# A sliding-window attention and channel-mix kernel: first loads in 512-byte runs, and a searched order of GpSimd's loads

## The chip, the cores and the metric

One core of a Trainium2 chip runs the whole program. The metric is device time in microseconds (us) of one execution; three runs of the kernel before gave a median of 232.38 us (231.59 to 232.47).

## The reference

```python
def _attn_ref(q, k, v):                     # q, k, v: (8, 8, 576, 64), float32
    scores = scale * np.matmul(q, k.transpose(0, 1, 3, 2))
    rel = pos[:, None] - pos[None, :]
    bias = slopes[:, None, None] * (-np.abs(rel))[None, :, :]
    mask = (rel >= 0) & (rel < 128)
    scores = np.where(mask, scores + bias[None], -1000000000.0)
    ...
    return np.matmul(attn, v)               # attn: softmax of scores

def _moe_ref(x, mu_k, mu_r, w_k, w_v, w_r): # x: (8, 576, 512), heads side by side
    x_prev = np.concatenate([zeros, x[:, :-1, :]], axis=1)
    xk = mu_k * x + (1.0 - mu_k) * x_prev
    xr = mu_r * x + (1.0 - mu_r) * x_prev
    k = np.maximum(xk @ w_k, 0.0)           # w_k: (512, 1024)
    v = k * k @ w_v                         # w_v: (1024, 512)
    return (1.0 / (1.0 + np.exp(-(xr @ w_r)))) * v
```

Causal attention over a window of 128 positions with a bias that falls with distance, and then a channel mix of its output.

## The kernel before

**The work.** Eight batches of 576 positions are four tiles of 128 and a tail of 64; the eight heads are four pairs. For a pair, q and k are brought to "head dimension on partitions" by transposes on TensorE (quarter-array ones at L1053, half-array ones at L804, or, for batches 6 and 7, by DMA transposes on SP's queue). Then come the scores (L693, 12 matmuls of 64 rows, the two heads side by side), their Exp on ScalarE (L707), a multiplication by a mask on VectorE (L720), and attend (L749, 18 matmuls against v with a column of ones, which gives the sums). VectorE divides (L755, L760), TensorE transposes back (L787, L804), a copy (L663) brings the result to `xt`, and VectorE makes the shifted mixes xk and xr (L847, L854). The channel mix runs in chunks of 256 to 512 positions: L958 (w_k), Relu on ScalarE (L965), the square (L929, L931), L976 (w_r), Tanh (L983), L992 (w_v), the product on VectorE (L997) and the store (L1022, the last piece L1016).

**The first batch** is done in two parts. Part 0 is its first 256 rows. `first_load` (L511) fetches q and k in float32 by SP's and ScalarE's hardware queues (L517) into `stage`. For pairs 0 and 1 a partition takes two neighbouring rows, which is a run of 512 bytes; VectorE casts them (L663 `qx<-qx`), and TensorE transposes them in bf16 (L1100). Pairs 2 and 3 (`FT`) come together, row by row, in runs of 256 bytes, and TensorE transposes them in float32 (L1097) with no cast. Part 1, the rest of the rows, is loaded by GpSimd. In this batch the bias goes in by matmuls (L680, `dist` and `sid`), whose operands GpSimd and VectorE make first: iota (L404), `ident` (L408), the cuts of `dist` (L412, L415), `sid` (L635), copies of `dist` (L633). All transposes need `ident`. Ninety matmuls on zeros (L654) fill TensorE while it waits.

**The order of work** is planned: each piece of work is a node with a duration, predecessors, buffers that it takes and gives back (`Hold`), and a priority for each engine. `Plan.run` (L106) places them one after the other, and each engine runs its list in that order. The priorities come from `rank` (L355), with fitted numbers in `LEAD` and `SHIFT`. `pe_key` (L98) lets pieces of 64 rows follow each other. The loads of GpSimd's queue are the exception: `dma` (L392) chains each to the one before, in the order of `LOADS`:

```python
    LOADS = 'vK23tVkabRcWw'
    ...
        n = plan.add(queue, issue, 0.0, list(deps) + [last.get(queue)],
                     (len(plan.nodes),), emit, need)
```

There v and V are halves of batch 0's v; K and k halves of w_k; 2 and 3 its part-1 q and k for heads 0 to 3 and 4 to 7; t the tails; a, b, c batch 1's q and k, tails, v; R is w_r; W and w halves of w_v. Batches 2 to 7 follow. Eight loads may be on the way at a time: the ninth waits for the landing of the first. Loads by GpSimd cast to bf16 on the way.

**Stores** go out from SP as 128 rows of 256 KB; the five tiles ahead of the last one go in two halves each. The last tile goes in 384 and 128 columns.

Of the kernel before, what the change touches and what calls it, by code (L numbers as in the profile page):

```python
# [10 lines left out]
BF16 = mybir.dt.bfloat16  # L11
# [22 lines left out]
class Plan:  # L34
# [148 lines left out]
def kernel(  # L183
# [14 lines left out]
    B, H, S, D = q.shape  # L198
# [29 lines left out]
    QUAD = 0.040  # L228
# [6 lines left out]
    WAIT = 0.0  # L235
    COST = {'first': 1.28, 'v': 1.15, 'q': 0.944, 'ts': 0.66, 'tv': 0.58, 'w': 0.88, 'run4': 1.0, 'run2': 1.03, 'flip': 1.0, 'mu': 1.0, 'x': 1.0}
# [14 lines left out]
    FT = (2, 3)  # L251
# [6 lines left out]
    KLAST = 1  # L258
# [71 lines left out]
    def dve_t(n, fast=1):  # L330
# [4 lines left out]
        PE: (46.3, 80.42, 22.29, 25.79, 41.56, 20.38, 22.23, 21.29, 23.26, 26.51),  # L335
        ACT: (-27.56, -45.55, 35.23, -5.26, -38.06, -61.17, 26.65, -81.7, -33.31, -34.13),
        DVE: (-18.77, -31.64, -26.58, 23.63, -67.49, 40.6, 13.9, -0.29, -44.69, 6.99),
# [3 lines left out]
        PE: {(0, 0): 84.89, (1, 0): -15.49, (2, 0): 37.21, (3, 0): 68.05, ('fkk',): -41.42, ('p1', 'fkk'): 6.29, ('p1', 'fxk'): 4.19},  # L341
        ACT: {(1, 0): -163.12, (2, 0): 31.31, (3, 0): 165.14, ('frl',): 21.61, ('rl', 'fp1'): 159.69, ('rs', 'fp1'): -160.42},
        DVE: {(0, 0): -143.93, (1, 0): 53.57, (1, 1): -50.21, (1, 2): -15.35, (2, 0): 32.09, (3, 0): -4.67, ('fp1', 'frs'): -48.4, ('frl',): -99.03, ('ot', 'fp1', 'frs'): -1.01},
# [11 lines left out]
    def rank(prio, need, free):  # L355

        if prio[0] == 0:
            _, b, part, g = prio[:4]
            k = 4 * b + g if b or part else g - 4
            step = (prio[4] if len(prio) > 4 else 9, prio[5] if len(prio) > 5 else 0)  # L360
            return {e: ((k - lead(e, min(k, 32))) * SLOPE + SHIFT[e].get(step, 0.0),) + tuple(prio)
                    for e in LEAD}
        if prio[0] == 1:
            what = tuple(sorted(h.cls for h in need)) + tuple(
                "f" + c for c in sorted({h.cls for h in free}))
            return {e: (prio[1] + SHIFT[e].get(what, 0.0),) + tuple(prio) for e in LEAD}
        return {e: (1e9,) + tuple(prio) for e in LEAD}
# [143 lines left out]
    def first_load(i, g, n):  # L511
        hs = (q, k)[i][0, 2 * g:2 * g + 2 * n]
# [5 lines left out]

        if g not in FT:
            st = stage[:, g:g + n].rearrange("p g i w -> p (g i w)").rearrange(  # L520
                "p (i h w) -> p i h w", i=2, w=128)
            return [put(155 * n, st[:, i], hs[:, 0:256].rearrange(
                "h (p r) d -> p h (r d)", p=128))]
        st = stage[:, g:g + n].rearrange("p g i w -> p (g i w)").rearrange(
            "p (i r h d) -> p i r h d", i=2, r=2, d=D)
# [3 lines left out]
    def staged(i, j, r):  # L529
        g = 2 if j > 1 else j  # L530
        n = 2 if j > 1 else 1
        st = stage[:, g:g + n].rearrange("p g i w -> p (g i w)")
        if g not in FT:
            return st.rearrange("p (i h r d) -> p i h r d", i=2, r=2, d=D)[
                :, i, 2 * (j - g):2 * (j - g) + 2]
        return st.rearrange("p (i r w) -> p i r w", i=2, r=2)[
            :, i, r, 128 * (j - g):128 * (j - g) + 128]
# [10 lines left out]
    for g, n in ((0, 1), (1, 1), (2, 2)):  # L548
        for i in range(2):
            x = first_load(i, g, n)  # L550
            for j in range(g, g + n):
                src0[i, j] = x
# [7 lines left out]
    def load_step(what):  # L560
        if what in "vV":
# [8 lines left out]
            if what == "V":  # L570
                vl[0].append(tv_load(0, vh[0], blank[0:4]))
# [28 lines left out]
    def batch_load(b, what):  # L600
# [15 lines left out]
        elif what == "c":  # L616
# [3 lines left out]
            vl[b].append(tv_load(b, vh[b]))  # L620

    for what in LOADS:
        load_step(what)
# [3 lines left out]
    for b in range(2, B):  # L627
        for what in "abc":
            batch_load(b, what)
# [262 lines left out]
    def tails(b, prio):  # L892
# [19 lines left out]
        t = op(PE, 0.03 * 16, list(tl[b]) + [n_ident], prio + (0,), emit, [hp], [hs])  # L912
        g = virtual("tt", [htt])
# [10 lines left out]
    n_hw = 39 + sum(4 if g in FT else 2 for g in range(3)) + 8 * len(XB) + len(XTT) + G * len(XO)  # L924
# [18 lines left out]
    def channel_mix(P, c0, c1, first, xks, xrs, order):  # L943
# [27 lines left out]
        for i, c in enumerate(range(c0 // 128, c1 // 128)):  # L971
# [30 lines left out]
            for a, b in ((0, FIN), (FIN, 512)) if final else ((0, 512),):  # L1002
# [42 lines left out]
    def qk_quad(b, g, nr, buf, deps, prio, c0, hq, take, free):  # L1045
# [13 lines left out]
        t.rows, t.lazy = (64, 64), True  # L1059
# [13 lines left out]
    for part in range(2):  # L1073
        if part == 1:
            htt, n_tt = tails(0, (0, 0, 1, 0))
        for g in range(G):
# [4 lines left out]
            elif part == 0:  # L1081
                cs = []
                for i in range(2):
# [3 lines left out]
                        staged(i, g, 0))))  # L1087
# [4 lines left out]
            def emit_t(e, part=part, g=g, hp=hp, f32=f32):  # L1092
                for i in range(2):
                    for r in range(2):
                        nn = 2 * i + r
                        if f32:
                            nc.tensor.transpose(one(hp)[:, 128 * nn:128 * nn + 128],  # L1097
                                                staged(i, g, r), id32)
# [7 lines left out]
            else:  # L1106
# [5 lines left out]
                    e, qk_buf[hq0[g].idx][:, :, 0:256],  # L1112
                    one(hp).rearrange("p (t c) -> p t c", t=2)) if f32 else copy_any(
                    e, qk_buf[hq0[g].idx][:, :, 256 * part:256 * part + 256].rearrange(
                        "p t (c r) -> p t c r", r=2),
                    one(hp).bitcast(BF16)[:, 0:512].rearrange("p (t r c) -> p t c r", t=2, r=2)),
                    (), [hp])]
            ha = Hold("at")
            es = []
            for j, (pieces, m0) in enumerate(PART[part]):  # L1120
                uses_tt = m0 == 512
# [4 lines left out]
                              ([hq0[g]] if part == 1 or True else []) + ([htt] if uses_tt else []))  # L1126
# [174 lines left out]
```

## Time and profile before

| | |
|---|---|
| median of 3 runs | 232.38 us |
| the profiled execution's own time | 232.61 us |
| its span, first to last instruction | 230.8 us |
| TensorE, matmuls busy | 221.1 us (96%) |
| VectorE, ScalarE, GpSimd busy | 186.9, 163.9, 93.7 us |
| granted TensorE clock | 1.0 throughout |
| GpSimd's DMA queue (q0) | 16.26 MB in 96,016 packets |
| SP's and ScalarE's queues (q1, q10) | 13.84 and 0.59 MB |
| first L1100, first L680, first L707 | 4.10, 5.55, 6.35 us |
| first L958, first L992 | 19.64, 37.44 us |

The page's part 2 cuts the span in 40 slices of 5.77 us and gives each engine's busy share in tenths. The warm-up matmuls count as busy there, so a 9 in the first three slices is not work. TensorE's records overlap: 128 columns are shown as 219 ns but follow each other every 56 ns, so the work is counted from the distance between starts. "Idle before" names what ended the wait. A DMA's "us to landing" runs from its issue to its end, and with eight loads on the way it is mostly time in the queue.

### The profile page before, as it was taken

Reading aid. Unit: us, or ns where it says so; the run is one execution under the profiler, and the core shown is the slowest. Engines: PE = TensorE matmul, PEld = TensorE weight load, DVE = VectorE, ACT = ScalarE, POOL = GpSimd, SP = SyncE. Lnnn points to the kernel's source line nnn. Section 1 sums busy time; section 2 is a strip of 40 time slices with the busy share of each in tenths; the row PEclk is TensorE's granted clock in tenths of the full one; section 3 lists DMA queues with packets and bytes.
Section 4 is the critical chain, followed back from the end, with each engine's and each line's share of the span. In section 5 each row is a group of like instructions: output and inputs, shape, how many; then the busy total and the mean of one; then the engine's idle time right before and its main releaser. Section 6 shows DMA issues by size and latency. Waiting matters only on the chain.

```text
span 230.8 us, 6660 instructions
## 1 busy us (share of the span) xinstructions
PE 221.1 (96%) x2682; PEld 134.3 (58%) x2715; DVE 186.9 (81%) x422; ACT 163.9 (71%) x296; POOL 93.7 (41%) x120
## 2 busy tenths in 40 slices
PE   7999998899999999999999999999999999999993
PEld 7575765665665755545665755545655654455562
DVE  7495998799977999899769998979999999343342
ACT  3769999489999977898897776964847516417260
POOL 8786655579869950686001990070000000000000
PEclk9999999999999999999999999999999999999999
DMA  6999999999999999989962999499723222121222
GB/s 169 182 163 194 189 158 200 200 167 151 201 147 169 171 125 167 119 82 175 227 98 70 179 151 206 93 122 169 128 57 121 67 82 76 46 92 45 69 70 91
DMA packets 121566, 31.11 MB, mean 135 GB/s; under 512 B 108216, under 2 KB 117696, under 8 KB 121536
## 3 DMA queue, kind: packets, MB, share of 16 engines
q0 software_dynamic: 96016, 16.26, 97.8%
q1 hardware_dynamic: 23776, 13.84, 25.1%
q10 hardware_dynamic: 1744, 0.59, 1.1%
q8 instruction: 21, 0.34, 0.6%
q14 instruction: 9, 0.07, 0.1%
HBM read 33.56 MB, written 9.44 MB: 186 GB/s over the span
## 4 chain that ended last, share of the span: by engine, by line
PE 77%; DMA 16%; issue 2%; POOL 2%; DVE 1%; ACT 1%; DVEq 0%; POOLq 0%; ACTq 0%
PE uno L992 25%; PE uno L958 25%; PE uno L976 12%; DMA wk_sb<-in_moe_w_k_dram 7%; PE duo L749 6%; PE duo L693 5%; DMA cb<-in_k_dram 5%; DMA vs<-in_v_dram 4%; PE uno L804 3%; POOL vs L467 1%; PE uno L1053 0%; DVE dl L847 0%; POOL tv L472 0%; PE uno L879 0%; ACT xt L663 0%
## 5 line engine op out<-in xcount | busy, mean ns | idle before, releaser
L958 PE MATMUL uno<-xk,wk_sb 128*128 128x256 bf16 (+2 forms) x413 | 70.8, 313 | 0.6 <-ACT qk L663 0.4
L992 PE MATMUL uno<-wv_sb,kk 128*128 128x512 bf16 (+2 forms) x282 | 69.5, 373 | 1.9 <-issue 0.8
L707 ACT ACTIVATE at<-duo 128x1024 bf16<-128x1024 f32 (+2 forms) x68 | 65.1, 1002 | 6.1 <-PE duo L693 5.3
L965 ACT ACTIVATE rl<-uno 128x256 bf16<-128x256 f32 (+2 forms) x104 | 47.4, 487 | 30.2 <-PE uno L958 27.0
L958 PEld LDWEIGHTS <-wk_sb 128*128 128x128 bf16 x416 | 38.5, 98 | 22.4 <-issue 0.4
L467 POOL DMA_DIRECT2D vs<-in_v_dram x32 | 28.5, 908 | 45.3 <-PE duo L749 37.2
L992 PEld LDWEIGHTS <-kk 128*128 128x128 bf16 x296 | 27.0, 98 | 27.7 <-issue 1.2
L720 DVE TENSOR_TENSOR at<-at,mask 128x1024 bf16<-128x1024 bf16 x56 | 37.3, 681 | 3.4 <-ACT at L707 3.4
L931 DVE TENSOR_TENSOR kk<-rl 128x256 bf16<-128x256 bf16 (+2 forms) x96 | 30.9, 336 | 9.9 <-ACT rl L965 8.8
L997 DVE SCALAR_TENSOR_TENSOR ot<-rs,uno 128x512 f32<-128x512 bf16 (+2 forms) x37 | 24.4, 667 | 13.8 <-PE uno L992 10.3
L976 PE MATMUL uno<-wr_sb,xr 128*128 128x512 bf16 x128 | 34.3, 379 | 0.8
L983 ACT ACTIVATE rs<-uno 128x512 bf16<-128x512 f32 x36 | 22.2, 628 | 11.7 <-PE uno L976 11.7
L663 ACT COPY qk<-uno 128x512 bf16<-128x512 bf16 (+1 forms) x42 | 22.6, 605 | 5.1 <-PE uno L1053 3.7
L854 DVE SCALAR_TENSOR_TENSOR xr<-dl,mu_sb,xt 128x576 bf16<-128x576 bf16 (+1 forms) x32 | 24.6, 777 | 0.0
L854 DVE SCALAR_TENSOR_TENSOR xk<-dl,mu_sb,xt 128x576 bf16<-128x576 bf16 (+1 forms) x32 | 24.3, 778 | 0.0
L760 DVE TENSOR_TENSOR xu<-duo,rc 128x640 bf16<-128x640 f32 x28 | 22.5, 813 | 2.1 <-PE uno L804 2.1
L749 PEld LDWEIGHTS <-at 128*128 128x128 bf16 x576 | 21.1, 98 | 5.1 <-issue 0.5
L976 PEld LDWEIGHTS <-xr 128*128 128x128 bf16 x144 | 13.6, 98 | 14.2 <-issue 0.2
L498 POOL DMA_DIRECT2D cb<-in_q_dram x20 | 17.7, 916 | 5.6 <-PE uno L804 3.2
L749 PE MATMUL duo<-vs,at 128*128 128x65 bf16 x448 | 18.7, 194 | 0.1
L498 POOL DMA_DIRECT2D cb<-in_k_dram x20 | 17.7, 916 | 2.2 <-PE uno L804 1.6
L663 ACT COPY xt<-uno 128x640 bf16<-128x640 bf16 (+3 forms) x28 | 15.1, 580 | 3.8 <-PE uno L804 2.4
(83 smaller groups left out, 200.3 us busy)
## 6 DMA issues: line engine op xcount, KB each, us to landing
out_dram<-ot SPq DMA_DIRECT2D x30, 256.0 KB, 4.1
vs<-in_v_dram POOLq DMA_DIRECT2D x32, 128.0 KB, 7.0
cb<-in_q_dram POOLq DMA_DIRECT2D x20, 128.0 KB, 6.1
cb<-in_k_dram POOLq DMA_DIRECT2D x20, 128.0 KB, 5.5
out_dram<-ot SPq DMA_DIRECT2D x10, 128.0 KB, 1.8
wk_sb<-in_moe_w_k_dram POOLq DMA_DIRECT2D x2, 512.0 KB, 7.5
cb<-in_q_dram POOLq DMA_DIRECT2D x4, 256.0 KB, 10.0
cb<-in_k_dram POOLq DMA_DIRECT2D x4, 256.0 KB, 10.4
```

The costliest lines, as they stand in the source:

```text
L467: return dma(POOL, 256, issue_t(1024), lambda e: nc.gpsimd.dma_start(out=vs_buf[h.idx][:, j, :, 0:D], in_=v[b, :, 128 * j:128 * j + 128].r ...
L498: return [dma(POOL, 256, issue_t(1024), lambda e, r=r: nc.gpsimd.dma_start(out=cb_buf[h.idx][:, i, r], in_=src[:, :, r]), [g], kind="q") f ...
L663: (nc.scalar.copy if e == ACT else nc.vector.tensor_copy)(out=out, in_=in_)
L707: lambda e, ah=ah, w=w, hp=hp: nc.scalar.activation(out=ah(), in_=two(hp)[:, :, 0:w], func=AF.Exp, scale=float(scale)), (), [hp])
L720: nc.vector.tensor_tensor(out=a, in0=a, in1=m, op=ALU.mult)
L749: nc.tensor.matmul(a[:, hl, t - t0], lhsT=at[:, lo:lo + 128], rhs=vs[:, u, 2 * g + hl, :] if u < NF else tvb[:, 2 * g + hl], start=(u == u ...
L854: lambda e: nc.vector.scalar_tensor_tensor(out=buf[hk.idx][:, g, e0 + c0:e0 + c1], in0=dls(), scalar=mu[:, g:g + 1], in1=xc(1), op0=ALU.mu ...
L931: nc.vector.tensor_tensor(out=out, in0=in_, in1=in_, op=ALU.mult)
L958: nc.tensor.matmul(one(hp)[:, 0:n], lhsT=wk_sb[:, po, 128 * fo:128 * fo + 128], rhs=xk_buf[hx.idx][:, po, c0:c1], start=(po == 0), stop=(p ...
L965: a = op(ACT, act_t(n), [s], pr, lambda e, hp=hp, hr=hr: nc.scalar.activation(out=rl_buf[hr.idx][:, 0:n], in_=one(hp)[:, 0:n], func=AF.Rel ...
L976: nc.tensor.matmul(one(hp), lhsT=xr_buf[hx.idx][:, po, 128 * c:128 * c + 128], rhs=wr_sb[:, po], start=(po == 0), stop=(po == NPO - 1))
L992: nc.tensor.matmul(one(hv)[:, a:b], lhsT=kk_buf[hk.idx][:, fo, o:o + 128], rhs=wv_sb[:, fo, a:b], start=(fo == 0), stop=(fo == NFO - 1))
```

## The change

- **First loads.** `FT` is empty: q and k of all four pairs come pair by pair, a partition with two neighbouring rows of each head (512 bytes); VectorE casts all of them, and all part-0 transposes are bf16. L1097 runs no more. The number of DMAs stays eight.
- **GpSimd's order.** With `PFREE` its loads and its three operations are no longer chained; their place comes from a table of keys, and the fabric's share of each load from a table of times (`LAND`). The list that results for the first loads: part-1 q (heads 0 to 3), the two tails, part-1 k (heads 0 to 3), two v tiles, **then iota**, part-1 q (heads 4 to 7), the two cuts of `dist`, the first half of w_k, part-1 k (heads 4 to 7), and then batch 0's other v tiles among batch 1's q and k, batch 1's tails, the second half of w_k, w_r, both halves of w_v, batch 1's v, batch 2's q and k with its tails among them.
- **The planner.** Quarter-array transposes and the tail's matmuls get a row class of their own (63, 127); `WAIT` is 1.64; `rank` gets tables for the first two batches and the first 28 pieces of channel mix (`FIRST`, `PAIR`, `MIX`), and `LEAD` and `SHIFT` have other numbers. So the order on TensorE, ScalarE and VectorE is another one throughout. On TensorE the first transposes stand behind 43 warm-up matmuls instead of 30.
- **Stores.** Five tiles are still stored in halves, but they end one tile earlier: the last but one goes out whole.

The diff, without the tables' numbers:

```diff
     def pe_key(self, n, rows):
-        if rows == 64 and n.rows[0] == 64:
+        if rows < 128 and n.rows[0] == rows:
             return (-1e8,) + tuple(key)
...
-    QUAD = 0.040
+    QUAD = 0.035
...
-    WAIT = 0.0
+    WAIT = 1.64
+    LAND = {
...
-    FT = (2, 3)
+    FT = ()
...
-    KLAST = 1
+    KLAST = 2
+    CUTOFF = 2
+    PFREE = True
+    P1JOIN = False
...
+            def at(e):
+                s = (k - lead(e, min(k, 32))) * SLOPE + SHIFT[e].get(step, 0.0)
+                if b < 2:
+                    s += FIRST[e].get((b, part) + step, 0.0) + PAIR[e].get((b, part, g), 0.0)
+                return s
+            return {e: (at(e),) + tuple(prio) for e in LEAD}
...
     def fab(queue, us, n, lat, free=(), flip=False):
-        us *= COST.get(getattr(n, "kind", None), 1.0)
+        us = LAND.get(getattr(n, "load", None), us * COST.get(getattr(n, "kind", None), 1.0))
...
+    PKEY = {
...
     def dma(queue, kb, issue, emit, deps=(), need=(), free=(), lat=(1.0, 0.9), flip=False, kind='x'):
-        n = plan.add(queue, issue, 0.0, list(deps) + [last.get(queue)],
-                     (len(plan.nodes),), emit, need)
+        free_ = PFREE and queue == POOL
+        n = plan.add(queue, issue, 0.0, list(deps) + ([] if free_ else [last.get(queue)]),
+                     (PKEY.get(group[0], 0.0) + place[0], len(plan.nodes)) if queue == POOL else (len(plan.nodes),),
+                     emit, need)
...
     def pool_op(dur, emit, deps=()):
-        n = plan.add(POOL, dur, 0.2, list(deps) + [(last.get(POOL), 0.0)],
-                     (len(plan.nodes),), emit)
+        n = plan.add(POOL, dur, 0.2, list(deps) + ([] if PFREE else [(last.get(POOL), 0.0)]),
+                     (place[0] - 0.5, len(plan.nodes)), emit)
...
-    def first_load(i, g, n):
-        hs = (q, k)[i][0, 2 * g:2 * g + 2 * n]
+    def first_load(i, g):
+        hs = (q, k)[i][0, 2 * g:2 * g + 2]
...
-        st = stage[:, g:g + n].rearrange("p g i w -> p (g i w)").rearrange(
-            "p (i r h d) -> p i r h d", i=2, r=2, d=D)
-        return [put(80 * n, st[:, i, r], hs[:, 128 * r:128 * r + 128].rearrange("h p d -> p h d"))
-                for r in range(2)]
...
+        return [put(155, stage[:, g, i].rearrange("p (h w) -> p h w", w=128),
+                    hs[:, 0:256].rearrange("h (p r) d -> p h (r d)", p=128))]
...
         t = op(PE, 0.03 * 16, list(tl[b]) + [n_ident], prio + (0,), emit, [hp], [hs])
+        t.rows = (127, 127)
...
-                        cut = (a, 256, b) if 0 < B * S - 128 - row <= 128 * n_split else (a, b)
+                        cut = (a, 256, b) if 128 * CUTOFF <= B * S - 128 - row < 128 * (n_split + CUTOFF) else (a, b)
...
-        t.rows, t.lazy = (64, 64), True
+        t.rows, t.lazy = (63, 63), True
```

More of the change, by code (lines that the diff above doesn't have):

```diff
@@ L234 @@
     NO = 5
[L235 to L236 removed]
+    WAIT = 1.64
+    COST = {
+        'first': 1.28, 'v': 1.15, 'q': 0.94, 'ts': 0.66, 'tv': 0.58, 'w': 0.88, 'run4': 1.0, 'run2':
+        1.03, 'flip': 1.0, 'mu': 1.0, 'x': 1.0,
+    }
+    LAND = {
[6 rows of a table added]
+    }
     SS = ()
@@ L365, in rank @@
                 "f" + c for c in sorted({h.cls for h in free}))
-            return {e: (prio[1] + SHIFT[e].get(what, 0.0),) + tuple(prio) for e in LEAD}
+            return {e: (prio[1] + SHIFT[e].get(what, 0.0) + (
+                MIX[e].get((prio[2] // 14,) + what, 0.0) if prio[2] < 28 else 0.0),) + tuple(prio)
+                    for e in LEAD}
         return {e: (1e9,) + tuple(prio) for e in LEAD}
@@ L547 @@
     src0 = {}
-    for g, n in ((0, 1), (1, 1), (2, 2)):
+    for g in range(G):
         for i in range(2):
-            x = first_load(i, g, n)
-            for j in range(g, g + n):
-                src0[i, j] = x
+            src0[i, g] = first_load(i, g)
     if KQ == ACT:
@@ L628 @@
         for what in "abc":
+            group[0] = str(b) + what
             batch_load(b, what)
@@ L922 @@
     of = out.rearrange("b s m -> (b s) m")
-    n_hw = 39 + sum(4 if g in FT else 2 for g in range(3)) + 8 * len(XB) + len(XTT) + G * len(XO)
+    n_hw = 39 + 2 * G + 8 * len(XB) + len(XTT) + G * len(XO)
     n_split = -n_hw % 8
@@ L1111 @@
                        lambda e, part=part, g=g, hp=hp, f32=f32: copy_any(
[L1112 to L1117, printed above, removed]
+                    e, qk_buf[hq0[g].idx][:, :, 0:256].rearrange("p t (c r) -> p t c r", r=2),
+                    (one(hp) if f32 else one(hp).bitcast(BF16)[:, 0:512]).rearrange(
+                        "p (t r c) -> p t c r", t=2, r=2)), (), [hp])]
             ha = Hold("at")
             es = []
+            if part and P1JOIN:
+                s, es = scores(0, g, [(pieces, m0, htt if m0 == 512 else None) for pieces, m0 in PART[1]], True,
+                               hq0[g], ha, ys + n_sid[2 * g:2 * g + 2] + n_tt + [n_dist] + list(n_copy.values()),
+                               prio, [ha], [hq0[g], htt])
             for j, (pieces, m0) in enumerate(PART[part]):
+                if part and P1JOIN:
+                    break
                 uses_tt = m0 == 512
@@ L1125 @@
                               [] if j else [ha],
-                              ([hq0[g]] if part == 1 or True else []) + ([htt] if uses_tt else []))
+                              ([hq0[g]] if part or not P1JOIN or True else []) + ([htt] if uses_tt else []))
                 es.append(x)
```

87 lines of the change are left out of this document (61 added, 26 removed), and 30 rows, old and new, of tables (FIRST, LAND, PAIR, PKEY).

## The prediction

> **What bounds the kernel now.** I read the slices of the page first, then the table of windows, then the chain, the waits and the timeline of the first 15 us.
>
> ```profile
> PE   7999998899999999999999999999999999999993
> DVE  7495998799977999899769998979999999343342
> ACT  3769999489999977898897776964847516417260
> DMA  6999999999999999989962999499723222121222
> ```
>
> TensorE is busy from end to end, and after slice 8 (46 us) no other row is. So the time is TensorE's own work plus what TensorE loses. I took that work from the spacing of matmuls in clean runs: 216 ns for 512 columns (eight L992 in 1.73 us in the chain), 163 for 384, 109 for 256, 29.4 for one L749, 56 for a 128-column transpose, 0.455 us for the 12 score matmuls of a head pair, and 0.095 us at each change of tile shape (to or from L693, L804, L1053, L906; none between scores and L804). Over the program's 2,715 matmuls, without the 90 warm-up ones (L654), that is 213.5 us with 110 changes. The last matmul ends at 227.2 us, so 13.7 us are lost. Place minus work done gives where: 4.1 us before the first transpose, 9.5 when the first L958 starts at 19.64, 10.2 at 28.3, 13.0 at 49.65, and only 0.7 in the 177 us after that. The change can win in the first 50 us or nowhere.
>
> ```profile
> core 0: us, PE busy (x) PEld busy (x) DVE busy (x) ACT busy (x) POOL busy (x), PEclk, DMA share, GB/s
> ...
> 10.00:15.00 5.00, 5.00 (x114) 4.33 (x113) 3.69 (x14) 3.06 (x7) 3.52 (x5) 1.00 1.78 176
> 15.00:20.00 5.00, 4.48 (x84) 2.23 (x85) 4.50 (x13) 4.65 (x11) 3.65 (x6) 1.00 1.82 173
> 20.00:25.00 5.00, 4.83 (x92) 3.73 (x90) 3.10 (x11) 5.00 (x15) 3.40 (x5) 1.00 1.52 191
> 25.00:30.00 5.00, 4.76 (x139) 3.79 (x135) 5.00 (x15) 4.94 (x15) 3.12 (x5) 1.00 1.75 184
> 30.00:35.00 5.00, 4.89 (x83) 2.84 (x72) 4.75 (x10) 5.00 (x8) 2.72 (x4) 1.00 2.28 160
> 35.00:40.00 5.00, 4.25 (x44) 2.55 (x40) 4.38 (x11) 5.00 (x12) 2.61 (x4) 1.00 1.33 201
> ```
>
> PE's 5.00 in the second row is warm-up filler, not work: its 5 us hold the last 42 of the 90. From 20 to 40 us ScalarE has no idle time: whatever delays its work early comes back as a wait of TensorE. Two waits are DMAs, both in the DMA-bound stretch:
>
> ```profile
> PE uno L992 <- DMA wv_sb<-in_moe_w_v_dram: 0.7, 1, 0.7
> PE uno L958 <- ACT qk L663: 0.4, 1, 0.4
> PE uno L1053 <- DMA cb<-in_k_dram: 0.3, 1, 0.3
> ```
>
> By place minus work these stand for 0.87 us at 37.4 (the first wv half) and, with ScalarE's copies of the late k behind the last, 1.2 us at 43 to 45.
>
> **The change, part by part.** The instruction orders of both programs show what moves.
>
> *Less work on TensorE.* Eight f32 transposes (L1097, spaced 109 ns) become bf16 ones (55 ns): -0.43 us. The new order has 115 changes of tile shape for 110: +0.48. Together +0.05.
>
> *First loads.* Four of the eight DMAs of q and k go from 256-byte to 512-byte runs. The two hardware queues moved 0.54 MB between 2 and 4 us (272 GB/s, mostly 512-byte, up to 358) and 0.46 MB between 4 and 6 (228, mostly 256-byte). For the 0.52 MB concerned, 2.1 us at 250 GB/s become 1.5 at 345: 0.6 us of DMA time saved, at least 0, at most 1. All that queues behind lands that much earlier.
>
> *GpSimd's order.* Its first instructions were iota (L404, 0.84 us) and the two cuts of dist; now six loads stand ahead of iota.
>
> ```profile
> 0.84 0.34 POOL L404 IOTA dist<- 128x256 bf16 x1 [0.39 <-POOLq L1285]
> ...
> 2.22 2.00 POOL L467 DMA_DIRECT2D vs<-in_v_dram  x2
> ...
> 5.69 0.77 POOL L463 DMA_DIRECT2D qx<-in_k_dram  x1
> ...
> 7.89 0.67 POOL L482 DMA_DIRECT2D ts<-in_q_dram  x1
> 8.52 0.65 POOL L482 DMA_DIRECT2D ts<-in_k_dram  x1
> ```
>
> The six (two qx 0.77, two ts 0.66, two vs 1.0) take 4.9 us, so iota ends at 6.0 us instead of 1.19. Behind it on VectorE wait ident (0.13) and everything after it in that queue: eight sid (0.15 to 0.2 each), id32, the copies of dist (0.77), and the casts of pairs 1 to 3. PE's first transposes need ident: 6.5 us for 4.10. Bias matmuls need the dist copies, which wait for sid and the cuts: about 8.9 for 5.55. Then 0.5 us of tv memsets, two casts (0.3 to 0.5 each), 1.3 us of memsets and two more casts come ahead of pair 3, so the fourth score block ends near 14.4 us instead of 10.4. In exchange q and k of the second row half, first in the queue now, land by about 9.2 us instead of 13.2 (issue 5.69 plus 7.5), and two of the four later score blocks move up to 15 and 16 us, where TensorE had filler. Following the order with full durations, I reach the end of the first batch's attends with 11.8 us lost, where before had 9.65: +2.15. Durations overlap in the trace (ScalarE's 256-column copies last 0.40 but start 0.28 apart, two L755 0.25 apart), and each of some ten handovers counted at full length is 0.1 too long: lower end +1.2. I take +1.2, the nearer to how the rows really follow each other, and keep both ends.
>
> By the Trainium skill, page "SBUF — State Buffer", section "SBUF: two separate sides", VectorE in a two-port mode shuts GpSimd out of the port through which it writes descriptors for its loads. Here the rows say little of it: the two vs issues beside VectorE's copies took 1.05 and 0.95 us, the mean of 32 is 0.908. By the rule in full, each of the three casts ahead of ident would stop the issues for its whole length; that case is priced below.
>
> *Loads later in the queue.* The batch-1 v (four vs and a tv, landing spread over 5.7 us by the trace, 29.99 to 35.66) goes behind both wv halves. So wv's second half lands near 39.95 - 5.7 - 0.6 = 33.7, its first near 31; TensorE asks for it at about 35. The 0.87 us goes. Batch-2 q and k keep their place but for two ts loads (0.4 each) among them; TensorE comes to them with 1.2 us less lost elsewhere, ahead of the wait by half a microsecond at least: I count the 1.2 us as gone, at worst 0.6 stays. What is late next is v itself: 39.95 - 0.6 = 39.3, needed at about 39.6 to 40. ScalarE's waits between 24 and 31 us (0.33 and 0.42): its work up to the first 1024-column Exp (L707, 29.80 us before) shrinks from about 20.2 to 18.7 us of spacing, since three Relus move behind; I let half of it go, -0.4.
>
> *Stores.* The last but one tile's store is one DMA again. Before, SP issued halves at 227.06 and 227.44 and the last tile's only at 227.96, though that was computed at 227.54. One issue less: last issue about 0.35 earlier. Two 256 KB stores at 203 to 207 us took 2.0 us each, so it lands before the last one. Against it: the last Tanh (L983) now waits for its rs buffer, and half of L992's 384-column part stands between it and the 128-column part that needs its PSUM tile: 1.0 us from R's matmuls to the free tile, 0.65 of matmuls between. -0.35 + 0.2: -0.15.
>
> Sum: +0.05 + 1.2 - 0.87 - 1.2 - 0.4 - 0.15 = **-1.4 us**. The profiled execution took 232.61 us (span 230.84 and 1.77 around it), 0.23 above the median of the runs, 232.38. So 231.2 against its own time, **231.0** as a median.
>
> **Rivals.**
>
> *A, the late start is free.* PE's losses to 14.6 us are covered by 90 warm-up matmuls either way, and the part-1 blocks moved up make the delay good: start +0.2 instead of 1.2, or all of the 2.8 us lost from 28 to 50 goes. 229.8. For it: DMA, not TensorE, ends the chain until 44 us. Against: ScalarE is full from 20 us on.
>
> *B, it cancels.* Start +2.15 and the waits as above: 232.0; with the 0.6 us at 43 us left, 232.6. For it: the walk with full durations.
>
> *C, slower: ScalarE falls behind.* Its first Exp starts at about 9.5 us instead of 6.35, and from there to 40 us it had no slack. If the first 1024-column Exp comes later than about 31 us, both duo tiles are held, and each further microsecond is TensorE's. At 3.1 us late (32.9): start 2.15 and 1.9 more, minus only wv's 0.87 and the stores: 232.38 + 3.1 = 235.4; at half that, 233.8, which I take as its price. Against it: the work ahead of that Exp is 1.5 us less.
>
> *D, GpSimd shut out.* Three casts of 0.42 us stop the issues: iota 1.25 later, all of it behind the first transposes: 232.3. By that page this is what would happen; the rows for vs speak for 0.1 us a piece.
>
> **How the numbers follow.** Forecast 0.50 (229.9 to 231.9 as its own range: 231.0 with the ends 0.6, -0.9); A 0.15, B 0.14, C 0.17, D 0.04. A measurement of this kernel tells about 0.5% (1.16 us) from no change. Faster than 231.2: three quarters of the forecast and A, 0.52. Within: the rest of the forecast, B and D, 0.30. Slower than 233.5: C and a trace of B, 0.18. The range reaches into A and over the middle of C: 229.2 to 233.6.
>
> **What would show it.** First transposes at 6.5 us (GpSimd's iota ending at 6.0); first Exp near 9.5; no wait of L992 for wv_sb; the first 1024-column Exp before 31 us (right) or after (C); wv ahead of vs in the landings; L749's first wait on vs_1, if any; the last store's issue less than 0.6 us after the last matmul. Wrong would be a fresh loss beyond 50 us, where the whole order of TensorE, ScalarE and VectorE is new and I price it at nothing because before lost only 0.7 there; up to 1 us of it is in the range.

## The result, and the profile after

The changed kernel takes 233.74 us (median of 22 runs, 233.39 to 234.45), the kernel before 232.43 beside it (22 runs, 231.59 to 234.5). The ratio is 1.0049, 95% interval 1.0033 to 1.0064: half a per cent slower, where 231.0 us were forecast. Ratios here and below leave disturbed runs out. The profiled execution took 233.65 us (span 231.87; before 232.61 and 230.84).

First a correction of the section on the change above: the first part-1 loads in GpSimd's new order are heads 4 to 7, and heads 0 to 3 come second. No number hangs on it.

TensorE's row in the slices of the page after the change (one slice is 5.8 us):

```profile
PE   7699889999999999999999999999999999999994
```

TensorE is full from the seventh slice on (before, from the ninth), and a 9 can still hide short waits. The account shows where the time goes. It is the same account as in the prediction: the place of a matmul in the trace minus the work that TensorE has done by then ("lost"). Here it is at four places that both programs have:

| place | lost before | lost after | new in this stretch |
|---|---|---|---|
| last attends of the first batch (21.67; 24.36 us) | 9.65 | 11.26 | +1.61 |
| the eight receptance matmuls (30.04; 34.23 us) | 10.61 | 13.83 | +1.61 |
| past the loads (49.65; 53.98 us) | 12.99 | 14.08 | -2.13 |
| last block of the channel mix | 13.73 | 14.69 | -0.13 |

The four sum to +0.96, and all of it is lost by 54 us. With 0.08 us more work, 0.2 in the last block and 0.22 less from the last matmul's end to the end of the span (3.50 before, 3.28 after) that makes the 1.03 us between the two spans.

The start, in the timeline of GpSimd after the change (start, length, line, tiles):

```profile
1.25 0.92 POOL L560 DMA_DIRECT2D qx<-in_q_dram  x1 [0.80 <-POOLq L1372]
...
4.19 1.78 POOL L564 DMA_DIRECT2D vs<-in_v_dram  x2
6.05 0.37 POOL L501 IOTA dist<- 128x256 bf16 x1
```

The six loads stand ahead of iota as forecast; they begin at 1.25 us, not at 0.84, so iota ends at 6.42. TensorE's waits after the change (line, what for, total, times, longest):

```profile
PE uno L1184 <- DVE ident L505: 1.4, 1, 1.4
...
PE uno L1184 <- DVE qx L746: 0.9, 2, 0.6
PE uno L1042 <- DVE qk L746: 0.7, 1, 0.7
PE uno L870 <- ACT rl L1049: 0.5, 1, 0.5
PE uno L1137 <- ACT xt L746: 0.4, 1, 0.4
```

No load is left among them: the waits for `wv_sb` and `cb` of before are gone. Behind the start, three waits for VectorE and ScalarE stand in their place. TensorE's timeline shows where (the bracket is the idle time before, and who ended it):

```profile
27.32 0.33 PE L870 MATMUL uno<-ident,xu 128*128 128x128 bf16 x3 [0.48 <-ACT rl L1049]
...
29.23 0.44 PE L1137 MATMUL uno<-ident,cb 64*64 64x64 bf16 x31 [0.43 <-ACT xt L746]
...
30.69 0.76 PE L1137 MATMUL uno<-ident,cb 64*64 64x64 bf16 x64
32.12 1.19 PE L1042 MATMUL uno<-xk,wk_sb 128*128 128x256 bf16 x8 [0.66 <-DVE qk L746]
```

In the account these places lose 0.64, 0.62 and 0.80 us, and 0.28 at 26.05. The three on the list wait for ScalarE or VectorE to empty one of the four one-bank PSUM tiles (`uno`), or for what is copied out of one. The table of windows, before and then after, tells the same without an account (10 us each; the first number is the window's length, the next three are PE, PEld and DVE, then ACT):

```profile
25.00:35.00 10.00, 9.65 (x207) 6.63 (x207) 9.75 (x24) 9.94 (x22) 5.84 (x9) 1.00 2.02 172
35.00:45.00 10.00, 8.53 (x156) 5.65 (x152) 8.56 (x18) 6.86 (x15) 5.29 (x8) 1.00 1.53 195
```

```profile
25.00:35.00 10.00, 8.42 (x197) 6.57 (x194) 9.40 (x26) 9.73 (x25) 4.21 (x6) 1.00 1.46 197
35.00:45.00 10.00, 10.00 (x113) 6.84 (x111) 9.84 (x22) 9.83 (x22) 6.53 (x10) 1.00 2.05 162
```

From 35 to 45 us TensorE is busy for 1.47 us more: the loads no longer hold it. From 25 to 35 it is busy for 1.23 us less: VectorE and ScalarE are about as busy as before, and TensorE gets less done beside them. The gain that was forecast came, and was paid for ten microseconds earlier and at the start.

### The profile page after: what moved, and what is told of

It reads as the page before. It is cut to its first block, busy times and chain, and to the rows that moved or that the text cites. A ratio compares the mean times of both kernels' runs of the same rounds, so it can differ in the third digit from the quotient of the medians.

```text
span 231.9 us, 6715 instructions
## 1 busy us (share of the span) xinstructions
PE 223.4 (96%) x2715; PEld 134.3 (58%) x2715; DVE 189.0 (82%) x422; ACT 165.0 (71%) x300; POOL 93.5 (40%) x120
## 4 chain that ended last, share of the span: by engine, by line
PE 91%; DVE 2%; ACT 2%; POOL 2%; issue 1%; POOLq 0%
PE uno L1042 28%; PE uno L1076 27%; PE uno L1060 14%; PE duo L776 7%; PE duo L832 7%; PE uno L887 3%; PE uno L1137 2%; PE duo L763 2%; PE uno L832 1%; ACT at L790 1%; POOL vs L564 1%; PE uno L737 1%; DVE sid L718 1%; POOL qx L560 1%; ACT xt L746 1%
## 5 line engine op out<-in xcount | busy, mean ns | idle before, releaser
L1076 PE MATMUL uno<-wv_sb,kk 128*128 128x512 bf16 (+2 forms) x296 | 70.8, 374 | 0.1
L1042 PE MATMUL uno<-xk,wk_sb 128*128 128x256 bf16 (+2 forms) x416 | 69.4, 314 | 0.7 <-DVE qk L746 0.7
L790 ACT ACTIVATE at<-duo 128x1024 bf16<-128x1024 f32 (+2 forms) x68 | 65.8, 1000 | 5.1 <-PE duo L776 5.0
L1049 ACT ACTIVATE rl<-uno 128x256 bf16<-128x256 f32 (+2 forms) x104 | 47.9, 494 | 15.8 <-PE uno L1042 13.9
L1060 PE MATMUL uno<-wr_sb,xr 128*128 128x512 bf16 x144 | 36.7, 379 | 0.0
L1015 DVE TENSOR_TENSOR kk<-rl 128x256 bf16<-128x256 bf16 (+2 forms) x91 | 29.8, 341 | 6.3 <-ACT rl L1049 4.7
L937 DVE SCALAR_TENSOR_TENSOR xr<-dl,mu_sb,xt 128x576 bf16<-128x576 bf16 (+1 forms) x32 | 24.4, 772 | 0.1
L937 DVE SCALAR_TENSOR_TENSOR xk<-dl,mu_sb,xt 128x576 bf16<-128x576 bf16 (+1 forms) x32 | 24.3, 775 | 0.0
```

The source lines that it names most:

```text
L790: lambda e, ah=ah, w=w, hp=hp: nc.scalar.activation(out=ah(), in_=two(hp)[:, :, 0:w], func=AF.Exp, scale=float(scale)), (), [hp])
L937: lambda e: nc.vector.scalar_tensor_tensor(out=buf[hk.idx][:, g, e0 + c0:e0 + c1], in0=dls(), scalar=mu[:, g:g + 1], in1=xc(1), op0=ALU.mu ...
L1015: nc.vector.tensor_tensor(out=out, in0=in_, in1=in_, op=ALU.mult)
L1042: nc.tensor.matmul(one(hp)[:, 0:n], lhsT=wk_sb[:, po, 128 * fo:128 * fo + 128], rhs=xk_buf[hx.idx][:, po, c0:c1], start=(po == 0), stop=(p ...
L1049: a = op(ACT, act_t(n), [s], pr, lambda e, hp=hp, hr=hr: nc.scalar.activation(out=rl_buf[hr.idx][:, 0:n], in_=one(hp)[:, 0:n], func=AF.Rel ...
L1060: nc.tensor.matmul(one(hp), lhsT=xr_buf[hx.idx][:, po, 128 * c:128 * c + 128], rhs=wr_sb[:, po], start=(po == 0), stop=(po == NPO - 1))
```

## The experiments

All ratios are to the kernel before, five rounds on one chip per group. Unless said otherwise the kernels compute all that the reference does.

### Late iota, and ScalarE's masks

Theory 1: the late iota is behind both losses. Theory 2: the later loss comes from ScalarE's order, where five masks (L1226) stand in a row from 25.3 to 27.0 us. Theory 3: the 512-byte loads or the added casts. In the first edit, iota, `ident`, the cuts, `sid` and the copies of `dist` go ahead of the plan's order:

```diff
-        for n in plan.run():
+        for n in iota_first(plan.run()):
...
+    def iota_first(order):
+        front = [n_iota] + first_sets + [n_ident, n_dist] + n_sid[0:2] + [n_idr] + n_sid[2:6] + list(
+            n_copy.values()) + n_sid[6:8]
+        return front + [n for n in order if n not in front]
```

> The changed kernel; iota, ident, the two cuts of dist, sid, id32 and the copies of dist go first on GpSimd and VectorE, as they stood before the change; every other order is the changed kernel's. Theory 1 (the late iota is the cause of both losses, at the start and at 26 to 33 us): first transposes near 5.0 us instead of 6.7 (43 warm-up matmuls still stand ahead), TensorE's loss at the first batch's late attends 9.9 us instead of 11.3, and the 2.6 us lost after it fall to about 1.1; median 231.0 to 231.8. Theory 2 (the loss at 26 to 33 us comes from ScalarE's new order, five masks in a row ahead of Relu and the xt copies): the start gains 1.3 us, the later loss stays near 2.6; 232.2 to 232.7. Theory 3 (512-byte loads and four more casts on VectorE are what is late): no change, 233.5.

Ratio 0.9983 (0.9957 to 1.0009). First transposes at 5.55 us instead of 6.71; lost at the first batch's last attends 9.2 instead of 11.26. Then come 0.28, 0.64, 0.62, 0.80 again, to the hundredth, only 2 us earlier. So the late iota, with all that waits for it, costs 2.05 us at the start, more than the whole loss there, and has nothing to do with the second loss. Half of Theory 1 falls. For Theory 3 nothing is left at the start, which with iota first is 0.45 us better than before. Not all of the 2.05 us reaches the end: the ratios differ by 0.66%, or 1.5 us. At 49.94 us this kernel loses 0.63 us where the changed kernel loses nothing; what it waits for there was not tried.

The start of this kernel also answers for the loads. With iota first GpSimd's first load is issued at 2.31 us, and the hardware queues' last two pairs land at 6.19 and 7.18 (q), 6.42 and 7.36 (k). In the changed kernel, same loads, GpSimd's from 1.25 us on, it is 7.22 and 8.34, 7.39 and 8.54. Before, with the short runs: 6.05 and 7.58, 6.44 and 7.83. The long runs save 0.4 us on the last pair; GpSimd's early loads cost it 1.2 us.

The masks go into ScalarE's idle time before 16 us, a few behind each of its first instructions: in the changed kernel, in it with iota first, and (with other counts) in the kernel before.

```diff
+        for after, count in ((4, 4), (7, 1), (10, 2), (12, 1)):
+            for m in reversed(todo[:count]):
+                rest.insert(max(rest.index(acts[after]), rest.index(n_dist)) + 1, m)
+            todo = todo[count:]
```

> The changed kernel; the eight mask activations move up in ScalarE's order into its idle time before 16 us (four behind the first qk copy, one, two and one behind later pieces). Theory 1: ScalarE is late because its first Exp is late, and masks are only 2.5 us of its work; little of the 2.6 us goes, 233.2 to 233.7. Theory 2: at 25.3 to 27.0 us five masks stand ahead of the Relu and xt copies that free TensorE's PSUM tiles; without them 1.2 to 2.0 us of loss go, 231.7 to 232.5.

Ratio 1.0047 (1.0029 to 1.0064), no different from the change alone. Of the four losses only the 0.62 shrinks, to 0.38. The 0.64 is there in full, in two parts (0.49 and 0.16), although ScalarE now stands idle for 1.31 us ahead of the Relu that TensorE waits for:

```profile
26.69 0.38 ACT L1049 ACTIVATE rl<-uno 128x256 bf16<-128x256 f32 x1 [1.31 <-PE uno L1042]
```

```profile
27.13 0.33 PE L870 MATMUL uno<-ident,xu 128*128 128x128 bf16 x3 [0.33 <-ACT rl L1049]
```

The Relu waits for the key product, and the transposes wait for the Relu. At this place, then, it is a chain of single results that holds TensorE, and not ScalarE's load of work.

> Both edits on the changed kernel. Theory 1: as the first edit alone, 231.0 to 231.8. Theory 2: both gains add, 1.3 and 1.2 to 2.0 us, 230.4 to 231.2, faster than the kernel before by 0.5 to 0.9%.

1.0005 (0.9982 to 1.0027); the same 0.64, 0.38, 0.80.

> The kernel before with its eight masks moved up into ScalarE's idle time before 14 us, nothing else. Theory 1: ScalarE there is not late, no change, 232.2 to 232.6. Theory 2: the losses of 0.3 to 0.6 us that TensorE has between 19 and 30 us behind ScalarE shrink by 0.5 to 1.0 in all, but the DMA waits at 37 and 43 us take most of it back, since they end by landings and not by work; 231.9 to 232.4.

1.0011 (0.9984 to 1.0038). Theory 2 falls, in both kernels.

### TensorE's runs of one kind

Theory 4: the new order puts 48 attends in a row, then 64 quads in a row; every 12 attends and every 16 quads (the quarter-array transposes) hold a one-bank PSUM tile until it is copied out, so a run takes all four. Theory 5: VectorE and ScalarE are full there, and TensorE's order only moves the wait. The edit writes the order of these pieces on TensorE out by hand and hands the four tiles out anew. In shorthand, not code (attends `av` of pairs A to D, transposes back `ot`, key products `k`, scores `sc`):

```diff
-quad32  avA avB avC avD  k  otA otB  k  tailf  otC otD  quad32  k  sc  quad64  k k  sc
+quad32  avA avB  k  avD  otA  k  avC  otB  tailf  otC otD  quad32  k  sc  quad64  k k  sc
```

> The changed kernel with the iota first, and TensorE's order altered in one stretch only: the four groups of 12 attends that end the first batch no longer stand in one run of 48, but are parted by the key products (4 matmuls) and copy-transposes that stood behind them; ScalarE and VectorE keep their orders. Theory 4 (each group of attends holds one of the four one-bank PSUM tiles until VectorE has divided it out, so a run of four groups leaves TensorE without a tile): the losses of 0.28 and 0.64 us at the two key products behind the attends fall to under 0.3 together, the later 0.62 and 0.80 stay, and the time is 231.5 to 231.9 us, against 232.3 with the iota first alone. Rival, Theory 5 (ScalarE and VectorE are full there, and TensorE's order only moves the place of the wait): the loss is 11.6 to 11.9 us again where the third group of scores of batch 1 has started, and the time is 232.2 to 232.5.

Ratio 1.002 (0.9995 to 1.0046) against 0.9983 with iota alone. Lost from the first batch's attends to 32 us: 3.3 us instead of 2.6. The waits are now smaller and more (0.15, 0.29, 0.37, 0.68, 0.34, 0.42, then the same 0.80).

> As the kernel before it, and the run of 64 quads is parted too: 32 quads, the 8 key matmuls that stood behind them, the other 32 quads; on ScalarE the two rectifiers of these key products go ahead of the copy of the later quads. One more pair of tile-shape changes, +0.13 us of TensorE work. Theory 4: the loss of 0.80 us at the 8 key matmuls also goes to under 0.3; lost at the eight receptance matmuls 10.7 to 11.1 us against 11.8; time 231.0 to 231.5. Theory 5: 232.2 to 232.6.

Ratio 1.0031 (1.0006 to 1.0057). The 0.80 at the 8 key matmuls is gone; 0.60 and 0.34 stand right behind it.

> As the kernel before it, and ScalarE's masks of the later batches go into its idle time before 16 us, as in the run with masks moved. Theory 4: the wait of 0.62 us behind the copies out of the copy-transposes falls to 0.4 or less as it did there, so 230.8 to 231.3; Theory 5: 232.2 to 232.9.

Ratio 1.0016 (0.9989 to 1.0043). Parting the runs moves the losses and takes none away. Theory 4 falls in the form in which it was put.

### The order of wv, and the halved stores

GpSimd's loads for batch 1's v go ahead of wv again, batch 2's q and k ahead of its tails, in the changed kernel with its late iota, and the halved stores are again the last (the first two lines are shorthand for the order of the queue):

```diff
-POOL:  w_r  w_v w_v  v v v v tv  q ts k ts q k
+POOL:  w_r  v v v v tv  w_v w_v  q k q k ts ts
...
-  cut = (a, 256, b) if 128 * CUTOFF <= B * S - 128 - row < 128 * (n_split + CUTOFF) else (a, b)
+  cut = (a, 256, b) if 0 < B * S - 128 - row <= 128 * n_split else (a, b)
```

> The changed kernel, iota late as it is, with two parts undone. GpSimd issues the loads of batch 1's v and its last rows ahead of wv, and batch 2's first q and k run ahead of its last rows, as before the change; and the halved stores are again the last ones. Theory 1 (the earlier wv is what took the 0.87 us wait and most of the 1.2 us wait away): by the landings in the changed kernel, wv as the sixth and seventh load of this stretch lands at 38.3 to 40.5 us, TensorE reaches its first use at 36.6, and waits 1.7 to 3.9 us there; the time is 235 to 237 us. Rival (wv's place is worth only what it cost before, since VectorE and ScalarE hold TensorE up in the same stretch): a wait under 1 us and a time of 233.7 to 234.6. Stores: 0.15 to 0.3 us more from the last matmul's end to the end of the span if the halves at the end cost that, under 0.1 if not.

234.63 us, ratio 1.0074 (1.0048 to 1.0099). The wait is back, in the list of waits and in the timeline:

```profile
PE uno L1076 <- DMA wv_sb<-in_moe_w_v_dram: 1.1, 1, 1.1
```

```profile
38.04 1.04 PE L1076 MATMUL uno<-wv_sb,kk 128*128 128x512 bf16 x4 [1.08 <-DMA wv_sb<-in_moe_w_v_dram]
```

The account has 1.15 us. I had expected 1.7 to 3.9, because I let TensorE wait for both halves; it needs only the first. So Theory 1's wait was too long, and the time came out at the rival's upper end. In the new order the earlier wv takes away a wait of 1.1 us; in time the two kernels differ by 0.25%, or 0.6 us, and their intervals overlap. The 1.2 us at batch 2's run don't come back: this kernel loses nothing from there to 55 us. In the new order TensorE comes to these quads only at 48.4 us here, and at 47.0 in the changed kernel, against 42.9 before; by 46.7 us the loads for them have landed here. The stores: 3.29 us from the last matmul's end to the end of the span, against 3.28. Where the halves stand makes no difference that these profiles show.

Now the place of wv in the kernel before, and only that (shorthand again):

```diff
-POOL:  w_r  v v v v tv  w_v w_v
+POOL:  w_r  w_v w_v  v v v v tv
```

> The kernel before with one change: GpSimd issues the two halves of wv ahead of the five loads of batch 1's v. What the prediction took: the wait of 0.87 us goes and the time falls by as much, to 231.5. Theory 5: TensorE comes 0.87 us earlier to the first quads of batch 2, whose load is not earlier, so the wait of 1.02 us there grows by most of it, and the time is within 0.4 us of the kernel before.

Ratio 0.9998 (0.9983 to 1.0014): nothing, where the prediction's term says 0.9963. Its waits:

```profile
PE uno L879 <- DMA ts<-in_k_dram: 0.5, 1, 0.5
PE uno L976 <- DMA wr_sb<-in_moe_w_r_dram: 0.5, 1, 0.5
...
PE uno L1053 <- DMA cb<-in_k_dram: 0.4, 1, 0.4
```

The wait for `wv_sb` is gone, and TensorE reaches the key product behind batch 2's quads at 44.36 us, where before reached it at 44.55. In this execution 0.5 us each went to `ts` and `wr`, whose loads stand ahead of wv and came 0.7 to 0.8 us later than in the profile of before; the 1.09 us at batch 2's run stand as they were (1.02). What exactly ate the gain differs from the mechanism that I wrote down; that nothing was left of it is what the time says.

### Adding and taking away work of VectorE

Three mixes of the token shift (L854 before, L937 after) are written twice between 26 and 31 us, once in the changed kernel with iota first, once in the kernel before:

```diff
+            if n.seq in TWICE:
+                n.emit(n.eng)
```

> The changed kernel with the iota first, and three token-shift mixes of VectorE between 26 and 31 us written twice (the same values, so 3 times about 0.46 us more of VectorE work there). Theory 5 (VectorE sets the place of TensorE from 24 to 36 us, and nothing later gives time back in the changed order): lost at the eight receptance matmuls 13.0 to 13.3 us against 11.8, and the time is 1.0 to 1.4 us over that of the iota first (232.3): 233.3 to 233.7. Theory 6 (the losses there are waits of single evictions for one another, with room on VectorE between them): under 0.5 us more, 232.3 to 232.8.

Ratio 1.0072 (1.0047 to 1.0097), by the two ratios 0.9% or 2.1 us over the kernel with iota first (each ratio is known to about 0.6 us). The wait at the 8 key matmuls grows from 0.7 to 2.0 us:

```profile
PE uno L1043 <- DVE qk L747: 2.0, 1, 2.0
```

A lower clock behind it adds the rest (below, in the last section). It didn't fall in every execution: two of the six had a mean clock of 1.0 and took 233.25 and 233.47 us, the other four (0.993 to 0.997) 234.55 to 234.92. Against the 232.2 to 232.3 of iota first, 1.4 us of added work costs about 1.0 to 1.3 us where the clock stays, as Theory 5 had it.

> The kernel before, with three token-shift mixes of VectorE between 26 and 30 us written twice, 1.4 us more of VectorE work. Theory 5, with what it says of the loads (the waits of 0.87 us for wv and 1.02 us behind the load of batch 2's first run, which the kernel before has at 37 and 44 us, are also time in which VectorE catches up): lost at 31 us 0.8 to 1.4 us more, but the two waits for loads shrink by about as much, and the time is under 0.5 us over the kernel before. Rival (the loads come on top of what VectorE loses): 1.0 to 1.4 us over it.

Ratio 1.0012 (0.999 to 1.0035). In the profile the lost time at 34 us is 13.06 instead of 10.70, of which 0.94 is a start that was late in this execution (a load of q); the other 1.42 is the added work. Then the wait for wv does not come at all, the 1.02 us at batch 2's run are 0.51, and at the key product behind it the kernel is 0.83 us later than before: less than its start was. In this execution the loads' waits have swallowed all 1.4 us; the time allows a cost of up to 0.8.

Then work is taken away. Copies of batch 1's first transposed q and k out of PSUM move a quarter of their columns: three on VectorE in the changed kernel with iota first, three in the kernel before, and at last all eight of the two engines.

```diff
-   e, qk_buf[hq.idx][:, :, c0 + w * r:c0 + w * r + w].rearrange("p t (c r) -> p t c r", r=nr),
+   e, qk_buf[hq.idx][:, :, c0 + w * r:c0 + w * r + w].rearrange("p t (c r) -> p t c r", r=nr)[:, :, 0:cut_c[0]],
```

> The changed kernel with the iota first, and work taken away from VectorE instead of added: three of its copies of batch 1's transposed q and k out of PSUM, between 27 and 33 us, copy a quarter of their columns (this leaves out three quarters of these three copies; the rest of the tile keeps what an earlier pair left there). A 512-column copy takes about 0.62 us of VectorE there, so some 1.2 us less work. Theory 5 (VectorE's work sets TensorE's place there): lost at the eight receptance matmuls 10.5 to 11.0 us against 11.8, and the time is 0.8 to 1.3 us under that of the iota first: 231.0 to 231.5 where the kernel before takes 232.6, a ratio of 0.993 to 0.995 against 0.998. Theory 6 (single evictions wait for one another): 0.4 us or less, a ratio of 0.997 or more.

Ratio 0.9995 (0.9969 to 1.0022). The 0.80 becomes 0.32; 0.28, 0.64 and 0.62 stay. Added work costs about its length, work taken away gives little: Theory 5 is half right.

> The kernel before with the same taken away: three of VectorE's copies of batch 1's transposed q and k, between 30 and 33 us, copy a quarter of their columns. Theory 5 with the loads as a second floor (batch 2's first run lands at 43 to 44 us whatever VectorE does, and TensorE needs it then): the time is within 0.4 us of the kernel before. If the loads do not hold it: 0.8 to 1.3 us under it.

Ratio 1.0008 (0.9983 to 1.0033): nothing, as Theory 5 had it.

> The changed kernel with the iota first, and work taken away from both evicting engines: all eight copies of batch 1's first transposed q and k out of PSUM (five on VectorE, three on ScalarE, between 22 and 33 us) copy a quarter of their columns; three quarters of these eight copies are left out. Some 2.1 us less of VectorE and 1.0 us less of ScalarE. Theory 7 (ScalarE and VectorE hold TensorE there together, so that relief of one alone only hands the wait to the other): 1.5 us or more of the 2.6 us that TensorE loses from 24 to 32 us goes, and the time is at least 1.0 us under that of the iota first on this chip. Rival (the order of TensorE's own pieces, each of which needs the result of the one before, sets the loss, whatever the two engines have to do): under 1.0 us goes there, and the time is within 0.5 us of the iota first.

> The changed kernel with the iota first once more, as the kernel to compare with on the same chip, and for a closer interval against the kernel before: 0.997 to 1.000 if the first result holds. Both theories expect the same of it.

0.999 (0.9966 to 1.0014) with all eight copies cut, 0.998 (0.9957 to 1.0004) without. Lost between 24.9 and 34.3 us: 0.28, 0.64, 0.62, 0.31, 0.15. With 3 us of work fewer on the two engines, the three waits are still on the list:

```profile
PE uno L1138 <- ACT xt L747: 0.4, 1, 0.4
...
PE uno L871 <- ACT rl L1050: 0.3, 1, 0.3
...
PE uno L1043 <- DVE qk L747: 0.2, 1, 0.2
```

0.5 us went of the 2.6, so the rival's numbers hold and Theory 7's don't. But this run says less than it seems to. Of the eight shortened copies only the first on each engine (25.07 and 25.12 us) stands ahead of the waits at 27.75 and 29.81; the other six come later. It shows that the last wait shrinks with the copies ahead of it (0.80 became 0.31). From the waits before that one it takes only some 0.7 us of work away, and it leaves VectorE's divisions as they were, which keep VectorE busy from 25.95 to 28.48 us. Both kernels with cut copies had a start that was 1.4 us late in the profiled execution (a load of `ts` at 8 to 10 us), which is upstream of the edit; the losses are compared within the stretch.

## Why the prediction was wrong

**The start, +1.2.** Right in its mechanism, short in its size: +1.61. Iota ended at 6.42 (6.0 forecast), first transposes 6.71 (6.5), first Exp 9.64 (9.5). The late iota alone is worth 2.05 at this place by a_iota; the rest of the new start is 0.45 us better than before. The measured 1.61 lies between the two ends of the walk, 1.2 and 2.15: some of its handovers did overlap, not all of them.

**First loads, 0.6 us saved.** 0.4 on the last pair when GpSimd starts as late as before; with its loads from 1.25 us on, the pair lands 0.7 us later than before. I had priced the shorter DMA time and not the six loads that now share it.

**ScalarE's waits, -0.4: the step that failed.** The stretch up to the eight receptance matmuls came out at +1.61. I counted ScalarE's work up to the first 1024-column Exp and found less of it; that Exp came at 30.99 us, just before the 31 us that I had set as the limit, and still this stretch lost 1.6 us more than before. With iota first it came at 28.96, earlier than the 29.80 of before, and the same 2.6 us were lost. So the count of work was the wrong measure. What the runs show of the cause: it is not the iota, not the masks (but for 0.24 us), and not the two long runs on TensorE by themselves. The last wait shrinks when the copies ahead of it are cut (r_dve, r_two). The wait of 0.64 is a chain: in a_masks ScalarE is idle ahead of the Relu, and the wait stays. What the runs leave for the rest is such a chain in the new order, from attends over VectorE's division, the transposes back and ScalarE's copies to a free PSUM tile. From 24 to 30 us TensorE has 12 key matmuls to put between its links where before had 24. That is read from the two orders and argued, not shown. VectorE's work on the divisions is a rival that no run touched, and which of the planner's new rules makes the order was not tried.

**wv -0.87 and batch 2's run -1.2.** Both waits went, and the stretch gave 2.13. The size is right; the reason is right for the wait for wv (p_old). The wait at batch 2's run stays away with the old order of the loads too; the new order brings TensorE there 4 us later, so that term came out by luck. And the terms did not stand beside the others as the sum had them. In the kernel before, the loads are a second floor under the same stretch: 1.4 us more of VectorE work cost 0.3 us there (-0.2 to 0.8), three copies fewer gave nothing measurable, and neither did wv alone moved forward (-0.4 to 0.3 us). Removing that floor is worth only what the engines above it can use, and the new order used up 1.6 us of it from 25 to 35 us.

**Stores, -0.15.** -0.22, but not for the reason given: undoing the halves' place changed 0.01 us. What is left is the new order of the last pieces, which was not tried by itself.

**Beyond 50 us** nothing new was lost, as forecast. Of the rivals, C's price of 233.8 is the nearest number, by luck: its Exp came no later than its limit, and the tiles that were held are the one-bank ones and not the two of Exp (`duo`). B (it cancels, 232.0 to 232.6) is too fast by 1.1 us or more, since it too had no new loss ahead of the loads. D: the six issues took 4.80 us beside three casts, against the 4.9 counted without any blocking. It was one cast that grew (0.96 us for 0.29): it began at 4.25, inside an issue that ended at 5.10, and ended at 5.22. Before has two such casts (0.60 and 0.47 us; issues ending at 4.22 and 4.98, casts at 4.31 and 5.09), and iota first one (0.69 us; 7.03 and 7.14). Other casts ran at 0.29 us inside an issue, so the overlap alone doesn't do it. By the Trainium skill, page "SBUF — State Buffer", section "SBUF: two separate sides", whichever of the two starts first keeps the shared port and the other waits. These casts agree with that, 0.09 to 0.12 us behind the issue's end; that a GpSimd issue waits for a cast, as D had it, is not seen in these rows.

A version better than both was not found for certain: the change with iota first stands at 0.9983 and 0.998 in two groups of runs, and both intervals reach 1.

## What to carry to other kernels

A wait for a load is a gain only if the engines above it have time to give; add work to them, or move the load alone, before the wait goes into a sum. When work is taken away as a test, see that it stands ahead of the wait in question. Where a whole order is new, follow the chain of single results through the few PSUM tiles; the totals of busy time do not show it. An operation on which all others of a start depend stays first in its queue, even if six loads could use its place.

## What the runs showed of the hardware

The kernel with doubled mixes shows what one long wait can cost beyond itself. The clock on record changes there at 32.74 and 36.15 us. In windows of that length, 3.41 us (the second number is PE's busy time, the third from the end the granted clock):

```profile
29.32:32.74 3.42, 1.45 (x27) 0.97 (x16) 3.38 (x8) 2.54 (x5) 0.86 (x2) 1.00 1.26 206
32.74:36.15 3.41, 3.19 (x20) 1.82 (x18) 3.41 (x10) 2.25 (x3) 1.44 (x3) 0.50 2.25 159
36.15:39.56 3.41, 3.41 (x28) 1.70 (x26) 2.19 (x5) 3.04 (x5) 2.11 (x3) 1.00 2.39 151
```

The wait of 1.97 us ends at 31.44. The clock stays at 1.00 until 32.74, is 0.50 for the next 3.41 us, and the account loses another 1.6 us. The kernel with eight cut copies shows the same at its start, behind a wait of 1.41 us and shorter ones:

```profile
7.05:10.46 3.41, 1.32 (x22) 0.75 (x22) 2.64 (x14) 1.40 (x2) 2.79 (x5) 1.00 1.97 169
10.46:13.88 3.42, 3.42 (x37) 1.53 (x36) 1.34 (x4) 1.99 (x3) 3.42 (x6) 0.50 1.47 199
```

In both, TensorE was busy for less than half of the window ahead of the fall. The changed kernel's idlest such window from 4.72 us on, 4.72 to 8.13 with a wait of 1.38, has 2.03 us busy, and the clock stays at 1.00; so it does behind the waits of up to 0.8 us from 20 us on. The clock's record begins at 5.43, 3.64 and 4.72 us of these three profiles, and its changes stand whole windows of 3.41 us behind that. If the windows begin at another point of the program in each execution, one and the same wait can fall into one window or be parted between two. That would fit the two of six executions that kept the clock; no run here tests it. The Trainium skill, page "TensorE: Matmul & The Clock Gate", section "HAM oscillation — how this bites in real kernels", warns of gaps beyond some 3.4 us; here a gap of 1.97 us was enough in a window that was otherwise partly idle.
